# A new issue order, with new engine choices, for a fused attention and two-MLP kernel

## The chip, the cores and the metric

The kernel runs on one core of one Trainium2 chip. The metric is the device time of that core in microseconds (us). The core's engines work side by side, each through its own queue in order: TensorE (PE in the profile), with its weight loads shown apart (PEld), VectorE (DVE), ScalarE (ACT), GpSimd (POOL), and SyncE (SP), which here issues every DMA.

## The reference

Attention with a threshold on the scores, then two dense blocks on the 2304 tokens. Everything is float32.

```python
# q, k, v: (4, 8, 576, 64)
scores = scale * (q @ k.T)
thresh = max(scores, -1) - tau
scores = where(scores >= thresh, scores, -1e9) - max
attn = exp(scores) / (sum(exp(scores)) + 1e-9)
x = attn @ v                          # -> x: (2304, 512)
# block 1: 512 -> 2048 -> 512
h = x @ w_in
g = (a0 + a1*h + a2*h^2 + a3*h^3) / (1 + |b0||h| + |b1|h^2 + 1e-6)
x = g @ w_out
# block 2: 512 -> 1024 -> 1024 -> 512
out = (((x @ w1) * (x @ w2)) @ w3) @ w_out2
```

## The kernel before

**Numbers in pairs.** Most products keep float32 accuracy by splitting each operand into a float16 head and a float16 remainder and doing three float16 matmuls in place of one. So after most results stand two elementwise steps: one that makes the head (`copy`, a cast or a scaled copy from one input), and one that subtracts the head from the value to make the remainder (`rest`, two inputs, both in SBUF).

**Work.** The kernel lists 2431 events in Python: loads, attention steps for 16 pairs of heads in two halves each (`qk`, `top`, `thr`, `below`, `drop`, `exp`, `recip`, `p_hi`, `p_lo`, `p_t`, `pv`, `x_split`), weight preparation (`raw_w`, `conv_w`, `square_w`, `norm_w`, `split_w`, `w_product`), and for nine groups of 256 tokens the first block (`mlp1`: per eighth `h_product`, `act_h`, `num`, `den`, `inv`, `quotient`, `y_product`) and the second (`mlp2`: `ab_product`, `a_copy`, `c_mul`, `o_product`, `o_store`). Many events are Python generators that stop between their steps, so that another event's instructions can come in between.

**The order is written out by hand.** `ORDER` (lines 31 to 234) is a text of 4124 entries. Each number calls the next step of that event, so the entry's place is its place in the queue of each engine that it uses, SP's included. A letter behind the number sets the engine of a step that may run on more than one: a is ACT, v is DVE, p is POOL; with no letter the step has DVE or a fixed engine.

```python
        for token in ORDER.split():
            n = int(token.rstrip("apv"))
            eng[0] = token[len(str(n)):]
            if n not in gens:
                fn, args, *_ = events[n]
                gens[n] = fn(*args)
            if gens[n] is not None:
                next(gens[n], None)
```

**The free steps.** Four helpers read that letter. `copy` (lines 285 to 294) makes heads and scaled copies, on ACT (L287, L289) or on POOL or DVE (L291, L293). `tt` (L303) is the two-input subtract, add or multiply of `p_lo` (tile hl), `split_w` (wp), `den` (A), the last step of `quotient` (gg from A and r) and the last of `c_mul` (gg from U), on POOL or DVE. `small` (L306) is the two-column arithmetic of `thr` and `recip`. When the head was made with a scale, `rest` is on DVE alone (L300). Only DVE and ACT of these three can read the matmul results, so `top`, `exp`, `num` and the like have a fixed engine.

**The lines that the prediction names.** DVE: L625, L628, L631 are the three integer steps of `conv_w` on a raw weight tile; L784, L786 `num`; L802, L804, L806 the first three steps of `quotient`, followed by the multiply at L303 that may go to POOL; L460 `top`; L492 the masking after `exp`. ACT: L473 `below`, which needs `thr`; L772, L776, L779 `act_h`; L794, L796 `inv`. PE: L480 `drop`, which adds the mask that `below` made; L451 `qk`; L765 `h_product`; L822 `y_product`, which reads gg; L929 `ab_product`; L961 `o_product`. Buffers are few: two each of the tiles U, A and r, three of gg, nine of G (which holds scores, heads and raw q and k).

Of the kernel before, what the change touches and what calls it, by code (L numbers as in the profile page):

```python
# [31 lines left out]
7 0 1 3 12 92 18 2 4 5 13v 22 8 94p 20v 10 15 24 26 27v 6 31 9 14 9 29 9 35 11a 33 17 37 17 11 39 53  # L32
40v 16a 19 40 17 55 42 23 16 42a 48 44p 57 28 48a 59v 61 50p 46 21 63 64 21 68 66 52 21 70 96 25 32
25 72p 72 25 74 98 74a 36 79 100 76p 30 30 102p 77 103 30 105 107 34 41 111 79p 81p 109 34 113 34
128 83 115v 65 115 38 116 237 129 116a 38 122 118p 38 122a 131 124p 120 45 43 85 43 133p 135 43 137
67 69 67 239a 67 139 87a 126 311 141 142 87 73 89 144 166 146v 146 154 47 73 47 148 47 71 80 170 71
148a 71 150p 172 73 132 90a 174 152 176v 154a 168v 90 179 73 155p 178 84 157 181 75a 82 82 82 183
134 185 149 134 187 134 241 189v 136 140 189 86 78 86 138 191 88 243 196 244 191a 246v 86 250 192p
88 151 248 158 151 194 151 88 143 95 143 143 88 99 252 91a 160 160 160 167 254 93 159 97 256 97 153
97 257 101 308 145 202 101 259p 161a 161 101 147 196a 156 104 259 162 49 198p 204 261 205 261a 207v  # L40
200 310 267 263p 164 104 164 211 310 267a 265 209 310 268p 213 169 316 104 217 169 51 169 104 51 54
51 175 58 106a 318 108 318 318 215 56 324 58 218 56 307 56 220p 177 184 58 177 177 220 180 110 326
272 326 222 228 309p 326 58 222a 274 125 228a 224p 276 171 278v 173 281 230p 226 182 60a 186 186 285
# [12 lines left out]
486 488p 382 491 387 382 376 301p 301p 382 490 438v 490 395 438 492 384 524 495p 494 509 496v 439
390 303p 524 390 439a 303p 498 390 509 398 441p 403 299a 398 305a 398 299p 499 442 511 497 411 502
305p 511 498 500 504 501 444 406 518 406 505 406 509 449 507p 507 444a 419 514p 501 508 543 501 513
446p 413 516 413 543 516 501p 447 413 527 520 508a 568 489 408 421 510p 421 513a 392 421 515p 400
451 427 452v 424 530 517 454 519 416 455 519 457 521 527 459v 523p 459 519 525 530 526 519p 528 429  # L60
460 529 429 460a 429 531 462p 471 432 576 527 435 533 532p 435 578 546 545 435 534p 535 548 561 473
548 574 534 443 579 475 536 547 561 581p 536a 571 443p 549v 541 443p 537v 440 437 476 541v 440p 542v
440p 463 582 573v 478 437a 586 544 535 437p 584 538 445 587 538 445a 538 448 445p 453 538v 589 448p
450 453v 448p 453v 450a 479 450p 546 481 550 546 552 554 465 551p 456 603 555v 555 467 557 467 483
456p 468 605 456p 553 607 792 591 484 608p 553 557v 592v 558p 503 592 512 594 470v 470 503 461 461a
594p 464 503 461p 595v 564 522 556 464a 560 540 564 464p 556 522 610 539 556 611 567 540 556p 564
567 466 569p 469 559 466a 559 469a 466p 458 469v 522 458a 794 472 540 458p 794 572 559 794 472a 484
# [1108 lines left out]
```

## Time and profile before

| | |
|---|---|
| median of 3 runs | 1206.86 us (1206.33 to 1208.5) |
| the profiled execution's own time | 1207.75 us |
| its span, from first to last instruction | 1206.0 us |
| mean granted clock of TensorE, share of full speed | 0.95 |
| bytes moved by the DMA queue | 119.05 MB |

The span is 1.75 us short of the execution's time. The busy shares of the engines are means over stages that differ: the weights are prepared and attention starts in the first part, attention runs beside both dense blocks in the second, and the last part is nearly dense blocks alone.

### The profile page before, as it was taken

What the parts mean: (1) busy time and instruction counts of PE and PEld (TensorE: products, weight loads), DVE (VectorE), ACT (ScalarE), POOL (GpSimd) and SP (SyncE); (2) the same over time, 40 slices, a digit from 0 to 9 for tenths busy, and PEclk for the clock granted to TensorE, in tenths of its full rate; (3) what the DMA queues carried; (4) which work ended last, traced back from release to release, by engine and by line L of the source; (5) the groups of instructions that cost most, each with busy time, mean ns of one, the idle gap of its engine ahead of it and who ended that gap; (6) DMA issues with size and microseconds to landing.
All of it is one profiled execution on the core that took longest, in us unless ns stands there. A gap on an engine that the chain in (4) does not pass through costs nothing. (4 is left out here: it accounts for less than half of the span.)

```text
span 1206.0 us, 20660 instructions
## 1 busy us (share of the span) xinstructions
PE 994.5 (82%) x7889; PEld 729.4 (60%) x7892; DVE 920.5 (76%) x1674; ACT 732.5 (61%) x1208; POOL 502.3 (42%) x452
## 2 busy tenths in 40 slices
PE   3687655679787677998799899889999998998998
PEld 2333333554555456767666776667677677777675
DVE  5889899798999889688878998887878757277201
ACT  6647877957868577767656666665556435355211
POOL 1314475753576475234543453353444213123111
PEclk9999676899889799999999999999999999999999
DMA  7988954465435534573445155314412510000000
GB/s 219 278 235 227 231 142 127 91 146 170 105 80 120 126 78 107 116 177 96 96 82 126 21 111 117 67 27 89 101 29 41 85 36 1 18 18 2 18 18 18
DMA packets 201443, 120.37 MB, mean 100 GB/s; under 512 B 176384, under 2 KB 180480, under 8 KB 201344
## 3 DMA queue, kind: packets, MB, share of 16 engines
q1 hardware_dynamic: 201344, 119.05, 40.6%
q8 instruction: 62, 1.02, 0.3%
q14 instruction: 37, 0.30, 0.1%
HBM read 69.21 MB, written 7.34 MB: 63 GB/s over the span
## 5 line engine op out<-in xcount | busy, mean ns | idle before, releaser
L822 PE MATMUL y<-gg,wp 128*128 128x256 f16 x1728 | 213.6, 277 | 38.2 <-POOL gg L303 31.0
L822 PEld LDWEIGHTS <-wp 128*128 128x128 f16 x1728 | 169.4, 99 | 78.2 <-issue 56.3
L765 PEld LDWEIGHTS <-wp 128*128 128x128 f16 x1728 | 171.2, 100 | 74.4 <-DVE U L786 24.6
L765 PE MATMUL h<-xp,wp 128*128 128x256 f16 x1536 | 189.2, 281 | 32.5 <-DVE U L786 20.1
L929 PEld LDWEIGHTS <-wp 128*128 128x128 f16 x1728 | 168.4, 98 | 34.0 <-issue 10.9
L303 POOL TENSOR_TENSOR hl<-p,hl 128x576 f16<-128x576 f32 x81 | 114.8, 1419 | 114.5 <-ACT hl L287 107.3
L303 POOL TENSOR_TENSOR A<-A,r 128x512 f32<-128x512 f32 x67 | 88.7, 1324 | 148.5 <-ACT r L779 148.3
L303 POOL TENSOR_TENSOR gg<-A,r 128x512 f16<-128x512 f32 x64 | 89.0, 1391 | 140.5 <-DVE A L806 104.3
L451 PE MATMUL S<-raw 64*128 64x288 f32 x472 | 103.9, 475 | 17.6 <-DMA raw<-in_k_dram 9.6
L460 DVE TENSOR_REDUCE m<-S 128x1 f32<-128x576 f32 x132 | 95.3, 749 | 17.1 <-PE S L451 11.9
L961 PE MATMUL y<-wp,gg 128*128 128x512 f16 x432 | 99.6, 379 | 1.4 <-ACT A L289 1.1
L929 PE MATMUL h<-yy,wp 128*128 128x256 f16 x768 | 90.9, 275 | 2.4 <-ACT U L289 2.2
L490 ACT ACTIVATE p<-S,m 128x576 f32<-128x576 f32 x88 | 63.3, 737 | 40.9 <-DVE m L460 29.7
L513 ACT ACTIVATE p<-p,su 128x576 f32<-128x576 f32 x84 | 64.0, 767 | 38.1 <-DVE su L508 37.9
L451 PEld LDWEIGHTS S<-raw 64*128 64x128 f32 x472 | 56.0, 205 | 48.1 <-issue 18.9
L303 POOL TENSOR_TENSOR gg<-U,gg 128x512 f16<-128x512 f32 x33 | 39.3, 1192 | 106.2 <-ACT gg L287 96.5
L802 DVE SCALAR_TENSOR_TENSOR gg<-U,cf,r 128x512 f16<-128x512 f32 x72 | 64.5, 896 | 17.3 <-ACT r L796 17.0
L772 ACT ACTIVATE U<-h,cf 128x512 f32<-128x512 f32 x72 | 55.5, 771 | 36.5 <-DVE A L806 16.3
L492 DVE SCALAR_TENSOR_TENSOR p<-S,th,p 128x576 f32<-128x576 f32 x88 | 70.0, 813 | 8.9 <-ACT p L490 6.7
L303 POOL TENSOR_TENSOR wp<-cw,wp 128x512 f16<-128x512 f32 x51 | 70.0, 1384 | 15.3 <-ACT wp L287 9.4
L786 DVE SCALAR_TENSOR_TENSOR U<-U,cf,h 128x512 f32<-128x512 f32 x72 | 53.5, 746 | 24.7 <-ACT r L779 18.8
L804 DVE SCALAR_TENSOR_TENSOR A<-A,gg 128x512 f32<-128x512 f32 x72 | 67.3, 935 | 5.8 <-DVE gg L802 0.5
(186 smaller groups left out, 1887.4 us busy)
## 6 DMA issues: line engine op xcount, KB each, us to landing
rw<-in_moe_w_dram SPq DMA_DIRECT2D x32, 512.0 KB, 4.0
rw<-in_moe_w_out_dram SPq DMA_DIRECT2D x24, 512.0 KB, 4.1
raw<-in_k_dram SPq DMA_DIRECT2D x32, 288.0 KB, 3.5
wr<-in_v_dram SPq DMA_DIRECT2D x16, 576.0 KB, 4.3
rw<-in_moe_w_in_dram SPq DMA_DIRECT2D x16, 512.0 KB, 4.4
wr<-in_v_dram SPq DMA_DIRECT2D x16, 320.0 KB, 3.1
out_dram<-A SPq DMA_DIRECT2D x16, 256.0 KB, 2.0
raw<-in_q_dram SPq DMA_DIRECT2D x16, 160.0 KB, 3.4
```

What stands on the lines that cost most here:

```text
L303: (nc.gpsimd if eng[0] == "p" else nc.vector).tensor_tensor(o, x, y, op=op)
L451: nc.tensor.matmul(t[s][:, half, :HS], x[r, o:o + 128], y[r, keys], start=True, stop=True)
L460: nc.vector.tensor_reduce(st["m", b, c, blk][:, s:s + 1], t[:, :, :HS], axis=AX.XY, op=ALU.max, negate=True)
L490: nc.scalar.activation(x, t, AF.Exp, bias=m)
L492: nc.vector.scalar_tensor_tensor(x, t, st["th", b, c, blk][:, s:s + 1], x, op0=ALU.is_ge, op1=ALU.mult, accum_out=su)
L513: nc.scalar.activation(p, p, AF.Copy, scale=su)
L765: nc.tensor.matmul(t[:, e, :], w[:, a, o:o + 128], x[:, y, c, :], start=c + i == 0, stop=c == KD - 1 and i == 2)
L802: stt(p[:, 0, :], u, cf[:, 3:4], r, ALU.add, ALU.mult)
L804: stt(t, t, QC, p[:, 0, :], ALU.add, ALU.mult)
L822: nc.tensor.matmul(t[j // 2][:, j % 2, :], w[:, a, 128 * j:128 * j + 128], x[:, y, TG * e:TG * e + TG], start=f + e + i + j % 2 == 0, stop ...
L929: nc.tensor.matmul(t[:, TG * e:TG * e + TG], w[:, a, o:o + 128], x[:, y, c, :], start=c + i == 0, stop=c == KD - 1 and i == 2)
L961: nc.tensor.matmul(st["o", g][kt], x[:, a, m:m + 128], w[:, y, :], start=jp + e + i == 0, stop=jp == 3 and e == 1 and i == 2)
```

## The change

Nothing but the text of `ORDER` changes. All 2431 events and all 4124 entries stay, so every instruction's operation, tiles and shape stay. Two things differ.

**Places.** Entries stand a little elsewhere. Counted from the two listings, over the steps that keep their engine, a step moves by about 2 places in its engine's queue on average on PE, ACT and DVE and by 1 on POOL; the largest moves are 19 on PE, 49 on ACT, 85 on DVE and 14 on POOL. In SP's queue an issue moves by 1.7 places on average, by 21 at most. All queues keep their number of matmuls and DMAs.

**Engines.** Counted from the two listings, over the whole kernel:

| step | before: ACT / DVE / POOL | after |
|---|---|---|
| `p_lo` subtract (hl) | 0 / 63 / 81 | 0 / 82 / 62 |
| `den` add (A) | 0 / 5 / 67 | 0 / 19 / 53 |
| `quotient` last multiply (gg) | 0 / 8 / 64 | 0 / 50 / 22 |
| `c_mul` subtract (gg) | 0 / 3 / 33 | 0 / 20 / 16 |
| `split_w` subtract (wp) | 0 / 5 / 51 | 0 / 14 / 42 |
| `p_hi` head from a scaled value | 64 / 4 / 16 | 47 / 6 / 31 |
| `p_hi` first step (scaled copy or scaled head) | 128 / 4 / 12 | 123 / 12 / 9 |
| `split_w` head | 30 / 4 / 22 | 22 / 7 / 27 |
| `c_mul` head | 32 / 0 / 4 | 23 / 6 / 7 |
| `split_v` head | 15 / 0 / 1 | 10 / 4 / 2 |
| `x_split` head | 31 / 1 / 0 | 26 / 6 / 0 |
| heads and copies of `a_copy`, `split`, `scale_q`, `w_evac` | 67 / 10 / 9 | 65 / 13 / 8 |
| `thr` and `recip` | 0 / 109 / 51 | 0 / 105 / 55 |

The diff, cut to its ends (206 lines are replaced by 206):

```diff
 ORDER = """
-7 0 1 3 12 92 18 2 4 5 13v 22 8 94p 20v 10 15 24 26 27v 6 31 9 14 9 29 9 35 11a 33 17 37 17 11 39 53
-40v 16a 19 40 17 55 42 23 16 42a 48 44p 57 28 48a 59v 61 50p 46 21 63 64 21 68 66 52 21 70 96 25 32
...
-2402 2403a 2393v 2392 2392 2402 2394 2394a 2390 2404 2394p 2390 2390 2395 2390 2395 2404a 2395 2404p
-2395 2400 2400 2400 2405 2400 2405 2405 2405 2407a 2406v 2406 2407
+0 7 1 12 3 18 92 2 4 5 13v 20v 22 8 10 94a 15 24 26 27v 6 29 9 19 9 31 9 33 37 11v 35 11 39 53 17 14
+17 40p 40 17 42 21 23 42a 21 48 21 44p 48a 55 28 57 50p 46 16a 59v 63 52 16 61 66 25 32 25 64 68 25
...
+2390 2390 2390 2401 2402 2402 2401 2403a 2393v 2394 2394v 2394v 2395 2395 2404 2395 2404a 2395 2404v
+2400 2400 2400 2405 2400 2405 2405 2405 2406a 2407a 2406 2407
 """
```

## Rows read from the trace of the kernel before

**Rows 1.** Busy time of each engine over the span, from the page.

```profile
PE 994.5 (82%) x7889; PEld 729.4 (60%) x7892; DVE 920.5 (76%) x1674; ACT 732.5 (61%) x1208; POOL 502.3 (42%) x452
```

**Rows 2.** Stages: length, busy us of PE, PEld, DVE, ACT, POOL; granted clock; DMA.

```profile
0.00:478.00 478.00, 330.86 (x2140) 215.90 (x2144) 419.14 (x707) 339.75 (x609) 246.75 (x227) 0.88 0.59 155
478.00:840.00 362.00, 327.31 (x2910) 251.42 (x2910) 296.76 (x584) 234.35 (x364) 151.24 (x137) 0.99 0.43 93
840.00:1206.00 366.00, 336.30 (x2841) 262.08 (x2839) 204.55 (x385) 158.37 (x237) 104.31 (x89) 1.00 0.16 34
```

**Rows 3.** Longest wait of DVE, 0 to 478: total us, times, longest.

```profile
DVE su L306 <- ACT p L495: 6.6, 5, 3.3
```

**Rows 4.** Longest waits of PE, 0 to 478.

```profile
PE S L480 <- ACT x L473: 39.3, 16, 9.7
PE y L822 <- POOL gg L303: 13.7, 7, 2.7
```

**Rows 5.** Longest waits of PE, 840 to 1206.

```profile
PE y L822 <- POOL gg L303: 10.2, 11, 1.8
PE h L765 <- ACT r L779: 5.3, 3, 2.8
```

**Rows 6.** Line 303 alone by stage: us busy (instructions) of DVE, POOL.

```profile
0.00:478.00 478.00, 11.71 (x12) 188.82 (x136) 0.88 0.59 155
478.00:840.00 362.00, 2.47 (x3) 120.29 (x90) 0.99 0.43 93
840.00:1206.00 366.00, 11.04 (x9) 91.53 (x71) 1.00 0.16 34
```

**Rows 7.** Line 303 on DVE: ns shortest/median/longest.

```profile
L303 DVE TENSOR_TENSOR gg<-A,r x8: 673/692/1640, 217.4 to 1072.8; 128x512 f16<-128x512 f32 x8
L303 DVE TENSOR_TENSOR A<-A,r x5: 1161/1298/1408, 873.5 to 1096.8; 128x512 f32<-128x512 f32 x5
L303 DVE TENSOR_TENSOR hl<-p,hl x3: 758/758/1044, 209.2 to 228.4; 128x576 f16<-128x576 f32 x3
```

**Rows 8.** Single-input heads: two by shortest/median/longest ns, one group.

```profile
L291 DVE CAST wp<-cw x4: 420/862/1372, 162.3 to 245.4; 128x512 f16<-128x512 f32 x4
L291 POOL CAST wp<-cw x22: 600/650/1487, 143.2 to 443.7; 128x512 f16<-128x512 f32 x22
...
L287 ACT ACTIVATE wp<-cw 128x512 f16<-128x512 f32 x30 | 18.0, 620 | 0.3
```

**Rows 9.** Timeline of POOL and of DVE, 701 to 703: start us, us.

```profile
701.23 1.70 POOL L303 TENSOR_TENSOR gg<-A,r 128x512 f16<-128x512 f32 x1 [2.09 <-DVE A L806]
...
701.92 1.56 DVE L804 SCALAR_TENSOR_TENSOR A<-A,gg 128x512 f32<-128x512 f32 x1
```

**Rows 10.** DVE lines, 0 to 478: busy us, mean ns.

```profile
L628 DVE SCALAR_TENSOR_TENSOR cw<-rw,cw 128x512 int32<-128x512 int32 x72 | 68.6, 952 | 2.0
L631 DVE SCALAR_TENSOR_TENSOR cw<-rw,cw 128x512 int32<-128x512 int32 x72 | 64.0, 890 | 1.8
L625 DVE TENSOR_SCALAR cw<-rw 128x512 int32<-128x512 int32 x72 | 50.3, 698 | 7.1 <-DMA rw<-in_moe_w_in_dram 3.6 <-DMA rw<-in_moe_w_dram 2.8 <-DMA rw<-in_moe_w_out_dram 0.8
...
L806 DVE SCALAR_TENSOR_TENSOR A<-U,cf,A 128x512 f32<-128x512 f32 x22 | 23.7, 1075 | 0.6
```

**Rows 11.** DVE lines, shortest/median/longest ns over the whole span.

```profile
L628 DVE SCALAR_TENSOR_TENSOR cw<-rw,cw x72: 669/693/1750, 17.3 to 409.4; 128x512 int32<-128x512 int32 x72
L631 DVE SCALAR_TENSOR_TENSOR cw<-rw,cw x72: 671/692/1740, 19.6 to 410.6; 128x512 int32<-128x512 int32 x72
L625 DVE TENSOR_SCALAR cw<-rw x72: 404/422/1501, 16.8 to 408.0; 128x512 int32<-128x512 int32 x72
L806 DVE SCALAR_TENSOR_TENSOR A<-U,cf,A x72: 731/752/1844, 186.5 to 1113.4; 128x512 f32<-128x512 f32 x72
L306 DVE TENSOR_SCALAR th<-m,d x58: 207/228/1327, 13.4 to 961.4; 128x2 f32<-128x2 f32 x44, 128x1 f32<-128x1 f32 x14
```

More of the change, by code (lines that the diff above doesn't have):

```diff
@@ new lines @@
+821 668 671 668 812 823 832 668 633 735 835 633 835 838 838 677 635a 846 674 674 841 674 633 659a
+846p 846v 841a 731 677 638a 688 841p 688 641 688 850 631 691 643 632 677 643 634p 643 636 649 844
+665 637 677 639 667 669v 695 640p 672 695 697 673 640 695 642 816 680a 850p 850p 844v 676 682 844v
+678 697 681 642p 644p 646v 683 697 662 685v 685 646 687a 645 817a 690 701 651 694 817 697 739 694a
+703 743 705 696p 710 707v 647 700a 710 699 702 650 648 712 706 648 712 714v 714 744 716a 736v 1186
+692 652a 736 724 706 652 655 724p 706 719 729 725p 660 704 729a 660 660 754 709 728 664 729p 726 670
@@ new lines @@
+901p 964 1000p 1074 1010 1032 909 960 901p 1032 1003 1032 1035 1003 1011p 969 904 1035 1038p 904a
+1011 1003 1022 1012a 904p 1051 1017 1023 1042 1022 1024p 1051 1042 1022 909p 1026 1022v 1027 1014
+1054 1025 1045 1054 1015 909p 1025 1028 1123 1045 1058 1054 1030p 1025 1058 1061p 1046 1045 1119
+1064 1047 1045p 1077 972 1064 1119 1077 1067 1077 1048 1030 1080 1083p 1031a 1048 1080 1017a 1033
+1086 1018p 1096 1086 1067 1034 1020 1067 1096 1067v 1090 1120 1048 1090 1099 1070 1262 1090 1099
+1070 1103 1090p 1122 1103 1099 1070 1189 1049 1122 1106p 1036 1122 1050v 1093 1037 1053 1128v 1037
@@ new lines @@
+1044 1039 1109 1424 1125 1109 1125 1052 1112 1131 1112 1055 1040a 1056 1057 1093 1112 1112v 1059
+1040 1192 1114 1060v 1060 1066 1602 1071 1066a 1062v 1063 1117 1068v 1192 1131 1072 1372 1069 1135
+1076 1141 1073 1075v 1078 1135 1093 1076 1141 1078 1079v 1089 1144 1079 1135 1085 1148 1115 1135p
+1085a 1148 1065 1115 1144 1087v 1124a 1091 1144 1088 1115 1092v 1199a 1196 1121 1094 1095 1196 1097
+1081p 1041 1082 1151p 1084 1154 1098v 1098 1209 1202 1100a 1154 1101 1138 1157 1202p 1202p 1043a
+1102 1209 1157 1157 1127 1157v 1107 1129 1130 1215a 1132v 1133 1104 1134 1108v 1108 1136 1105 1137
@@ new lines @@
+1241 1179v 1179 1672 1180 1181a 1223 1421 1182 1241 1224 1184 1226 1229 1188 1227v 1230 1229 1230
+1232v 1232 1233a 1242 1190v 1222 1190 1238 1235 1244 1238a 1243 1236 1239p 1245v 1244 1246 1248
+1247v 1250 1185 1249 1240 1250v 1234p 1234p 1221 1250v 1319a 1251p 1269 1187 1675 1187 1251 1252a
+1319 1221 1254 1611 1237 1271 1221 1273 1276 1255 1237 1274v 1278 1276 1237 1237 1278 1259 1279v
+1279 1281a 1286 1283 1286a 1427 1253 1288v 1261a 1263 1253 1261 1290 1253 1285 1265 1257a 1256 1265
+1257 1265 1429a 1270 1374a 1268 1268 1253 1268 1270 1260a 1268 1260 1268 1291 1258 1272 1374 1258
@@ new lines @@
+1603 1287 1275 1608 1275 1272 1677 1287 1293 1272 1295 1277p 1298 1266 1337 1297v 1289 1298 1289
+1292 1289 1337 1292 1300 1321 1294p 1280 1300 1304 1280 1267v 1296 1282 1302p 1304 1296 1282 1322a
+1282 1282v 1481 1324 1306 1299 1306 1284 1299 1306 1284 1299 1311p 1302 1299v 1309 1284 1309a 1308
+1301 1313 1308 1310p 1301 1313 1326 1609 1312 1316 1320 1303a 1605 1316 1305 1320 1316 1331 1307
+1316v 1301 1323 1327 1318 1323 1325 1329p 1323 1318 1325 1340 1331 1606 1318 1328p 1342 1333 1371
+1342 1330 1333 1330 1371 1340 1334v 1332 1340 1332 1346 1344v 1332 1347 1354 1348 1347 1332p 1334
@@ new lines @@
+1349 1354 1341 1336a 1349 1341p 1353 1335 1349 1343p 1356 1335 1349v 1356 1359 1356 1352 1359 1373
+1361p 1352 1350 1373 1373 1351v 1376 1314 1355 1378v 1742 1364 1376 1380 1338 1380 1335 1364 1353
+1339 1315a 1345 1352 1355 1426 1357v 1357 1383 1363 1383 1426 1383 1366 1383p 1379 1431a 1366 1388
+1613 1315 1366 1614 1366v 1388 1381 1382 1386 1363p 1365p 1358p 1367 1368 1384v 1387 1368 1360 1386
+1362 1390 1390 1368 1387 1390 1385 1395v 1389p 1401 1389 1397 1392 1385 1396 1392 1396a 1375 1391v
@@ new lines @@
+1474a 1472 1536 1474 1546 1488 1536 1476a 1548 1551 1476 1549v 1488 1552 1540 1551 1552 1509 1491
+1554v 1554 1491 1494 1509 1491 1494 1560 1497v 1564 1512 1500 1515 1537 1500 1515 1512 1503 1512
+1503 1518p 1529 1539a 1503 1539 1521 1529 1566 1503p 1521 1567 1570 1560p 1550 1523 1532 1569p 1532
+1523 1561p 1506 1532 1523 1506 1555a 1535 1572 1523p 1550 1557 1526 1535 1553 1558 1526 1570 1553
+1553 1556 1506 1556 1542p 1538p 1541 1559p 1526 1541 1572 1571 1562 1544 1573p 1562 1544 1592 1573
+1544 1579 1544v 1575a 1571 1579p 1565 1547 1576 1563 1581p 1574 1547 1565 1574 1578 1582 1574 1565
@@ new lines @@
+1751 1696 1673 1756 1715v 1700p 1673 1717 1702p 1674 1701 1900 2143 1701a 1753 1701v 1758 1754p 1707
+1703 1756 1676a 1676 1718 1799a 1724 1758 1759v 1704 1759 1726 1761a 1720p 1704 1727v 1766 1721v
+1710 1763 1729 1723 1799 1704 1765 1707 1729 1730v 1730 1704 1732a 1771 1713a 1733 1710 1773 1775
+1778 1746 1766p 1768p 1739 1716 1780 1716v 1776p 1855 1716v 1735 1778 1719 1741a 1770 1743 1747v
+1719 1780 1719 1782v 1782 1741 1719 1788 1745 1722 1745 1745 1748 1788a 1722 1748 1748 1725 1728a
+1748 1783a 1748 1750 1785 1790p 1792 1725 1787 1750 1731 1731a 1736 1752 1731v 1804 1752 1738 1755
@@ new lines @@
+1738 1752 1755 1767 1679a 1805 1757p 1807 1767 1811 1809v 1760 1679 1734 1760 1811 1769 1734 1762
+1812 1957 1734 1762 1734 1762 1794 1740a 1812 1762p 1740 1772 1772 1814p 1737a 1826 1795a 1814 1737
+1821 1795 1764 1828 1784 1829 1769 1769 1831v 1784 1833 1816p 1821v 1774v 1857p 1833 1823p 1777 1801
+1777 1817 1786 1764 1779 1819 1786 1779 1786 1824 1764 1779 1834 1791p 1801 1779v 1793 1834 1781
+1793 1836v 1789 1781 1803 1789 1800 1803 1781 1796 1803 1818 1796 1808p 1796 1818 1810 1796v 1810
+1836 1806 1843 1798 1806 1820 1838p 1798 1813 1820 1820 1835 1822 1802p 1813 1825p 1835 1822 1827
@@ new lines @@
+1984 1924p 1985 1988 1931 1987v 1990 1988 1946a 1914 1990 1973a 1954 1991v 1974 1991 1936 1997 2002
+1956a 1958 1956 1914 2004 2024 1966 2005v 2007 1993v 1997p 1999v 1961 2007 1977a 1966 1961 1979p
+1961 1914 1964 1926 1980 1964 2008p 1976 1943 1964 1943 1964 1964 2025 2008 1948 2010a 1948v 1986
+1948v 2000 2027 1969 1986 2011 1969 1969 1972 1914 2031 2021 1972 1975p 1926 1936a 1994 1926 1936p
+1978 1926 2028 1996 1978 2006 2030v 2033 1981 1989 2022v 1938 1981 1989 1938 1981 1989 1938 1981v
+1995p 1938 1992 1950 1992 1998 1950 2031 1998 2017 2033 2034v 2034 2001 2041 2001 1950 2019a 2001
@@ new lines @@
+1950 1953a 2019 2006 2001v 1953 1955a 2088 2009 1955 2012 2026 2012 2009 2090 2026 2009 2092 2095
+2013 1983 2015v 2093p 2029 2095 1983 2018 2032 2018 2003 2032 2096 2003 2020 2029 2029 2096 1983
+2035v 2098p 2003 2098 2037 2020 2046 2104 2020 2037 2020v 2014 2040 2046 2036a 2016 2040 2016 2040
+2066 2049 2040v 2049 2038 2066 2049 2052 2099a 2039 2052 2045 2069 2101 2069 2023 2047 2069 2043
+2048 2051 2023 2050v 2055p 2102 2074p 2057 2072 2057 2051 2043 2053 2041p 2060 2042p 2023 2060 2043
+2077 2077 2044 2060 2086 2060v 2053 2063 2072 2063 2054p 2080 2080 2063 2080 2086 2080v 2054 2106
@@ new lines @@
+2089 2089 2091 2106 2089 2091 2061 2094v 2109 2061a 2056p 2058 2097 2062p 2148 2059 2110 2108 2108
+2112 2083 2097 2111 2113p 2108 2083 2111 2115 2104p 2100 2105p 2116 2145 2100 2114p 2100 2145 2117
+2100v 2083 2117 2115 2103 2151a 2120 2103 2064 2120 2120 2103 2120v 2065 2116 2148 2087 2118v 2118
+2124 2129 2154 2154a 2123 2130 2123 2067 2154p 2068v 2070 2132p 2123 2126a 2070 2081 2133 2071v 2071
+2128a 2133 2131 2135v 2135 2136a 2084 2119p 2121 2157 2107 2122 2124a 2134 2138 2157 2082a 2134
+2125p 2139 2157 2134 2157 2140 2137a 2160 2073v 2075 2137 2085a 2147 2160 2082 2149 2165a 2162 2150
@@ new lines @@
+2152 2155 2076 2162 2153v 2156 2155 2156 2174 2168 2174 2168a 2168v 2078 2171 2079 2079 2158p 2158
+2159a 2141 2127 2164 2169 2161 2164a 2171 2170 2166p 2171 2142 2175 2172 2142 2188 2167 2173v 2176
+2175 2188 2176 2178v 2178 2184 2171 2194a 2180v 2144 2184v 2186v 2179a 2181 2191 2146a 2163 2146
+2177 2191 2177 2197 2183 2197a 2187 2189 2182 2197p 2182a 2363 2190 2192v 2182p 2193 2363 2193 2195v
+2185 2195 2196a 2185 2198 2185 2199 2200 2204 2185 2206a 2206 2199 2199 2199 2201 2205a 2207 2203
+2205 2368 2203 2208 2217 2202a 2208 2208 2202 2209 2210 2209 2209 2217 2209 2209 2210 2368 2211 2211
@@ new lines @@
+2212 2364 2211 2212 2218 2213v 2224 2218 2219 2214 2219 2214 2224 2218 2215 2215 2220p 2245 2215
+2221 2245 2215v 2225 2225 2216 2226 2225 2216 2226 2221 2227v 2231 2222 2228 2222 2228 2222 2231
+2222v 2229 2216 2232 2229 2223 2233 2364 2233 2229 2223 2229v 2246 2223 2246 2247 2230 2246 2247
+2230 2232 2248v 2232 2249 2238 2249 2238 2234v 2235 2235 2236 2230 2236 2252 2236 2236v 2239 2252
+2239 2240 2239 2240 2237 2241v 2237 2242 2237 2242 2259 2243 2243 2243 2369 2250 2253 2243p 2259
+2250 2253 2250 2244 2253 2250v 2244 2254 2255p 2254 2244 2256 2251 2256 2273 2257 2257 2251 2257
@@ new lines @@
+2257v 2273 2258 2275a 2258 2260 2260 2261 2274 2260 2261 2262v 2274 2263 2263 2283 2276 2264 2283
+2264 2264 2278 2264v 2265 2265 2278 2266a 2251 2280a 2258 2276a 2265 2276v 2279 2267a 2268 2285v
+2279 2269 2281 2277 2269 2284 2269 2271 2270a 2284 2270 2288 2286 2295 2286a 2281p 2281p 2288 2286v
+2289 2290a 2289 2296 2277 2291 2297 2277 2297 2297 2282 2299 2277 2299 2282 2291a 2299 2282 2291p
+2282 2298a 2299 2299 2287 2287 2298 2287 2287 2362 2292 2292 2292 2292 2300 2294a 2293v 2293 2294
+2300 2307 2301 2302 2301 2307 2301 2302 2303v 2314 2308 2304 2309 2314 2304 2309 2308 2305 2308 2369
@@ new lines @@
+2305 2310p 2305 2328 2305v 2311 2311 2328 2315 2312 2315 2316 2306 2315 2306 2316 2317v 2312 2306
+2318 2312 2321 2318 2312v 2329 2319 2321 2329 2319 2329 2319 2313 2331p 2319v 2313 2322 2332 2330
+2313 2322 2323 2320 2322 2323 2320 2332 2330 2324p 2335 2325 2325 2335 2326 2326 2342 2326 2326v
+2336 2342 2333 2336 2337 2336 2327 2333 2338p 2327 2333 2339 2333v 2320 2339 2337 2327 2343 2340
+2334 2343 2344 2334 2343 2344 2345p 2340 2340 2346 2340v 2346 2334 2349 2349 2347 2347 2341 2350
+2347 2341 2350 2347v 2350 2351 2348 2370a 2351 2352p 2348 2371 2353 2378 2353 2354 2378 2354 2354
@@ new lines @@
+2341 2354v 2365a 2348 2366 2379 2366a 2366v 2355 2380a 2355 2355 2356a 2373 2357a 2358 2374 2374
+2367 2367 2367 2367 2379 2373 2381 2381a 2371p 2371p 2372 2375a 2381v 2372 2376 2372 2376a 2372
+2376v 2359 2377 2359 2359 2377 2361 2360a 2377 2408 2377 2385 2360 2382 2382 2382 2382 2409 2384a
+2383v 2383 2384 2409 2414 2411a 2414 2415 2416a 2415 2410 2417 2417a 2419 2417v 2419 2410 2420 2412
+2412a 2420 2412v 2413 2413 2413 2418 2413 2418 2418 2418 2424 2425 2425 2424 2426a 2421v 2422 2396
+2427 2396 2427a 2422p 2422p 2427v 2423 2398a 2423 2423 2423 2428 2428 2428 2428 2386 2430a 2429v
@@ L232 @@
+2429 2430 2387 2387 2386 2397 2388a 2389 2397 2391 2399 2399a 2389p 2389p 2392 2399v 2391 2392 2390
+2390 2390 2390 2401 2402 2402 2401 2403a 2393v 2394 2394v 2394v 2395 2395 2404 2395 2404a 2395 2404v
+2400 2400 2400 2405 2400 2405 2405 2405 2406a 2407a 2406 2407
 """
```

290 lines of the change are left out of this document (94 added, 196 removed).

## The prediction

> **What bounds the kernel now.** I read the page's busy line first, then the busy time by stage, then the waits of DVE and of PE in each stage, and last the durations on line 303 and of the DVE instructions that run beside it. No engine is full over the span: PE is busy 82%, DVE 76%, ACT 61%, POOL 42% [rows 1]. A mean over the span hides three stages, so I cut both listings where 30% and 65% of PE's matmul work has been issued; in the trace of before these places fall near 478 and 840 us. From 0 to 478 DVE is the fullest: 419.14 of 478 us, 88%, with PE at 330.86 (69%) and a granted clock of only 0.88 [rows 2]. The 59 us in which DVE is idle there are scattered: its longest wait in sum is 6.6 us in 5 times [rows 3]. PE's long waits in this stage, 39.3 us of `drop` for `below` and 13.7 us of `y_product` for gg [rows 4], stand behind work that DVE or POOL does late. So I take DVE to set the pace of the first stage. From 478 to 840 PE is at 327.31 of 362 us (90%), DVE at 296.76 (82%); from 840 on PE is at 336.30 of 366 (92%), DVE at 204.55 (56%) [rows 2]. There PE sets the pace, and what it loses it loses in short waits, the largest of them 10.2 us in 11 times for the gg that POOL makes [rows 5].
>
> **The change part by part.** It removes and adds no instruction; it moves 101 two-input steps of line 303 from POOL to DVE (19 hl, 14 A, 42 gg of `quotient`, 17 gg of `c_mul`, 9 wp), and some thirty single-input heads from ACT to POOL and DVE.
>
> *What a moved step costs DVE.* On DVE, line 303 takes 0.692 us for gg and 0.758 for hl in the median [rows 7]. For A only five rows exist, 1.161 to 1.408 us, all beside POOL; the lower bound is the 0.673 of gg, which has the same 512 elements, the upper the 1.298 of the median [rows 7]. I take 0.69, since the row of the same size that ran alone is the nearest. On POOL the same line takes 188.82 us for 136, 1.39 us each [rows 6].
>
> *What a removed step gives DVE back.* POOL does not work beside DVE for nothing. In the timeline POOL starts a subtract at 701.23 that lasts 1.70 us, until 702.93; DVE's L804, begun at 701.92, lasts 1.56 us and ends just after it [rows 9], more than twice the 0.692 of a two-input step of this size in the median [rows 7]. The `conv_w` steps show the same over the first stage: L628 has a mean of 0.952 us against its shortest of 0.669, L631 0.890 against 0.671, L625 0.698 against 0.404, each 72 times, and L806 1.075 against 0.731, 22 times [rows 10, 11]. The excess is 72 x (0.283 + 0.219 + 0.294) + 22 x 0.344 = 57.3 + 7.6 = 65 us of DVE time. POOL did 136 instructions of line 303 in that stage [rows 6], so one of them holds DVE for about 0.48 us. That is a mean of what collided, and its bounds are 0 (the steps left on POOL collide with the newly arrived ones instead, which read two tensors of SBUF too) and the full 1.39 us of the instruction. Even a two-column step of `thr` that takes 0.228 us lasted up to 1.327 [rows 11].
>
> The Trainium skill (SBUF — State Buffer, section "SBUF: two separate sides") says that GpSimd and those VectorE instructions that read two SBUF tensors lock one port pair for a whole instruction and that the loser blocks fully. The pair of instructions at 701 us agrees. By that rule taken to its end each removed POOL step would give DVE back its whole 1.39 us, and the first stage below would come out at -14 us; by my mean of 0.48 it comes out at +13. This is the first rival.
>
> *First stage.* 30 of the steps leave POOL (10 hl, 3 A, 8 gg, 9 wp) and 29 arrive on DVE: 9 x 0.758 + 20 x 0.69 = 20.6 us. Ten or so heads and scaled copies arrive as well (`split_v`, `split_w`, `x_split`), at 0.42 us for a 512-element cast that ran alone [rows 8], and some two-column steps, in all about 7 us. Sum +27.6. Given back: 30 x 0.48 = 14.4. DVE's load rises by 13 us, to 432; the ends are +28 (nothing given back) and 27.6 - 30 x 1.39 = -14. If DVE keeps its 59 us of idle time, the stage becomes 13 us longer. But the order brings some relief: entries of `drop` that stand closer behind their `below` than that step's duration, by the matmuls between them, fall from 40 to 30 in the two listings, and remainders made on DVE land 0.7 us sooner than on POOL. I let that take 5 us of idle time: **+8**, ends -14 and +28.
>
> *Second stage.* 32 leave POOL, 33 arrive: 9 x 0.758 + 24 x 0.69 = 23.4, other steps about 9, given back 32 x 0.48 = 15.4. DVE goes from 297 to 314 us of 362, 87%; PE with 327 remains the fuller one. What covers the added work is DVE's idle 65 us there. If that cover is gone, that is, if DVE's steps come late to a PE that has only two buffers of U, A and r ahead, the ends are 0 and +12. I take **+2**.
>
> *Third stage.* 39 leave POOL, among them 22 of the 23 multiplies of `quotient`. DVE goes from 205 to at most 205 + 39 x 0.69 + 2 = 234 of 366 us (64%), which costs nothing. The gg that PE waits for comes 1.39 - 0.69 = 0.7 us sooner, on 11 waits 7.7 us. But the new listing also places `y_product` and `o_product` closer behind their gg: in the last quarter of the matmul work, steps of `o_product` with fewer matmuls between them and their gg than the producer lasts were 6 and are 13, those of `y_product` were 15 and are 9. I count half: **-4**, ends -8 and +3.
>
> *Moves at no cost.* ACT loses 51 steps of about 0.62 us [rows 8]; ACT at 61% is not the bound in any stage [rows 1, 2], so nothing follows. Fifteen more `p_hi` heads go to POOL at about 0.65 us [rows 8]: POOL is at 52% in the first stage [rows 2] and has lost more than it gets; what covers them is that idle half. The DMA issues keep their number; SP's queue is reordered by 1.7 places on average, so a transpose may stand one issue later, and the DMA engines are busy 59% at most [rows 2]. In the first entries the loads of tau, a and b go ahead of the first v load; that is a microsecond at most of a first wait. The last two output copies both run on ACT, in place of one each on ACT and DVE; the first of them can run while PE does its last matmuls. I cost all of these at nothing.
>
> **Sum.** 8 + 2 - 4 = +6 us on the profiled execution: 1207.75 + 6 = 1213.75. The median of the runs shown is 0.9 below the profiled execution, so about 1213.
>
> **The rivals.**
>
> *The port rival, on the other side.* The price of a POOL step to DVE decides the first stage. It breaks even at 27.6 / 30 = 0.92 us per step removed. For a dearer price speak the 1.70 and 1.56 us pair [rows 9] and the longest rows of 1.75 us [rows 11]; against it that medians lie within 0.03 us of the shortest [rows 11], so most DVE instructions are not held. With the price at 1.2 the first stage is 27.6 - 36 - 5 = -13, the second 0, the third -4: 1207.75 - 17 - 0.9, about 1190.
>
> *The latency rival, also faster.* DVE would not be the pace of the first stage but the chain from subtract to transpose to the next matmuls would. Then a third of the 53 us of the two waits in [rows 4] goes with the shorter lead: -17 + 8, with the third stage -4, about 1194. Against it: DVE's longest wait is 6.6 us of 478 [rows 3].
>
> *No change.* DVE's idle 59 us take the 13 us in and the third stage loses nothing: 1205 to 1209.
>
> *DVE becomes the bound in the second stage as well.* For it speak 87% against PE's 90%, with shallow buffers. It gives +18 in the first stage, +12 in the second, 0 in the third: about 1237.
>
> **How the numbers follow.** The forecast (1209 to 1222) has 0.34, the port rival 0.28, the latency rival 0.12, no change 0.14, the double bound 0.12. A measurement of this kernel tells 0.2% (2.4 us) from no change. So faster has 0.28 + 0.12 = 0.40, same 0.14, slower 0.34 + 0.12 = 0.46; the forecast is the likeliest single case. The range has to hold cases of both signs: it runs from the port rival's 1190 to 1232, below the double bound's middle; beneath it I leave about 0.1, above it about 0.1. The forecast's own range is 1209 to 1222.
>
> **What would show it.** Right: DVE busy near 960 us over the span (920.5 + 13 + 17 + 39 x (0.69 - 0.48) + 2) and near 432 in the part that does the first 30% of the matmuls; POOL near 378 (502.3 - 101 x 1.39 + 24 heads of 0.65); mean of L628, L631 and L625 lower, but by less than a tenth of a us each; the PE wait of `y_product` for POOL's gg in the third stage down from 10.2 us to below 3. Wrong on the port price: DVE's busy time in the first stage at or below 419 though it does 29 more subtracts. Wrong on the pace: DVE's load up as said, but its idle time in the first stage down from 59 to 40 us or less. Wrong in the second stage: DVE above 90% there and PE waits for U or gg grown.

## The result: 0.9% faster, where 0.5% slower was forecast

The changed kernel takes 1196.9 us (median of 4 runs, 1195.8 to 1197.25) against 1206.69 for the kernel before beside it: a ratio of 0.9914 [0.9897, 0.9932]. The profiled execution took 1197.16 us with a span of 1195.4, 10.6 us less than before. So the time lies in the range on record, but the forecast had the wrong sign: 6 us slower on the profiled execution was forecast.

The page's busy line of the changed kernel answers to [rows 1].

```profile
PE 988.0 (83%) x7890; PEld 728.4 (61%) x7892; DVE 973.5 (81%) x1802; ACT 699.9 (59%) x1157; POOL 388.9 (33%) x375
```

DVE does 128 instructions more and is 53 us longer busy, and the kernel is faster all the same. The stages, cut again where 30% and 65% of the matmul work has been issued, answer to [rows 2]: length, busy us of PE, PEld, DVE, ACT and POOL, granted clock, DMA.

```profile
0.00:470.00 470.00, 329.35 (x2164) 218.06 (x2167) 427.45 (x751) 330.72 (x596) 207.07 (x204) 0.88 0.62 158
470.00:830.00 360.00, 321.44 (x2882) 247.55 (x2881) 322.59 (x635) 217.64 (x337) 124.52 (x118) 1.00 0.43 96
830.00:1195.40 365.40, 337.25 (x2846) 262.75 (x2844) 223.45 (x418) 151.57 (x227) 57.32 (x55) 1.00 0.16 32
```

These cuts are rounded. For a finer cut I matched the instructions of each kernel with those of before, in order, so that every stage holds the same share of the matmul work. By that matching the first stage ends 9.9 us earlier, the second is 2.3 us shorter and the third 1.6 us longer: -10.6 in sum. Cut by the number of weight loads alone, the three come to -10.0, +0.6 and -1.2, so the signs of the last two are not settled. Forecast were +8, +2 and -4. The gain is made in the first stage; the granted clock there is 0.88 in both kernels.

PE's longest waits there answer to [rows 4].

```profile
PE S L480 <- ACT x L473: 31.7, 11, 12.4
PE y L480 <- ACT x L473: 16.9, 6, 9.4
...
PE y L822 <- POOL gg L303: 7.3, 5, 2.2
```

`drop` waits for `below` 48.6 us in its two forms; before it was 39.3 for the first of them [rows 4] and 12.6 for the second:

```profile
PE y L480 <- ACT x L473: 12.6, 6, 4.0
```

The wait of `y_product` for POOL's gg fell from 13.7 [rows 4] to 7.3. DVE's longest wait in that stage was 6.6 us [rows 3] and is now 3.5:

```profile
DVE m L460 <- PE S L451: 3.5, 5, 1.3
```

The third stage's longest waits of PE answer to [rows 5]. POOL's gg has gone from 10.2 us to 1.9, and 8.9 us for DVE's gg stand in its place, so the wait for gg has not become shorter. The wait for U rose from 3.1 us to 6.9.

```profile
PE y L822 <- DVE gg L303: 8.9, 9, 1.9
PE h L765 <- DVE U L786: 6.9, 7, 1.6
PE y L822 <- POOL gg L303: 1.9, 1, 1.9
```

Line 303 by stage (busy us of DVE, then POOL) answers to [rows 6], and its shortest, median and longest durations on DVE to [rows 7]. The A step, of which before had five rows of 1.16 us and more, takes 0.684 in the median: the lower bound was right.

```profile
0.00:470.00 470.00, 36.53 (x43) 152.03 (x107) 0.88 0.62 158
470.00:830.00 360.00, 27.30 (x33) 76.27 (x57) 1.00 0.43 96
830.00:1195.40 365.40, 35.82 (x49) 43.19 (x32) 1.00 0.16 32
```

```profile
L303 DVE TENSOR_TENSOR gg<-A,r x50: 676/691/1695, 203.8 to 1104.3; 128x512 f16<-128x512 f32 x50
L303 DVE TENSOR_TENSOR hl<-p,hl x22: 744/758/864, 29.9 to 943.0; 128x576 f16<-128x576 f32 x22
L303 DVE TENSOR_TENSOR A<-A,r x19: 678/684/694, 256.5 to 1069.0; 128x512 f32<-128x512 f32 x19
```

The `conv_w` lines in the first stage (busy us, mean ns, idle before) answer to [rows 10]. Two of the three means fell, L628 by 0.08 and L625 by 0.13 us, and that of L631 rose from 0.890 to 0.916.

```profile
L631 DVE SCALAR_TENSOR_TENSOR cw<-rw,cw 128x512 int32<-128x512 int32 x72 | 65.8, 916 | 1.8
L628 DVE SCALAR_TENSOR_TENSOR cw<-rw,cw 128x512 int32<-128x512 int32 x72 | 62.7, 872 | 2.1
L625 DVE TENSOR_SCALAR cw<-rw 128x512 int32<-128x512 int32 x72 | 41.0, 570 | 5.4 <-DMA rw<-in_moe_w_in_dram 2.7 <-DMA rw<-in_moe_w_out_dram 1.4 <-DMA rw<-in_moe_w_dram 1.3
```

### The profile page after: what moved, and what is told of

It reads as the page before. It is cut to its first block, busy times and chain, and to the rows that moved or that the text cites. A ratio compares the mean times of both kernels' runs of the same rounds, so it can differ in the third digit from the quotient of the medians.

```text
span 1195.4 us, 20542 instructions
## 1 busy us (share of the span) xinstructions
PE 988.0 (83%) x7890; PEld 728.4 (61%) x7892; DVE 973.5 (81%) x1802; ACT 699.9 (59%) x1157; POOL 388.9 (33%) x375
## 5 line engine op out<-in xcount | busy, mean ns | idle before, releaser
L765 PE MATMUL h<-xp,wp 128*128 128x256 f16 x1536 | 192.5, 284 | 32.8 <-DVE U L786 17.7
L303 POOL TENSOR_TENSOR A<-A,r 128x512 f32<-128x512 f32 x53 | 74.1, 1400 | 187.4 <-ACT r L779 152.2
L303 POOL TENSOR_TENSOR hl<-p,hl 128x576 f16<-128x576 f32 x62 | 88.2, 1423 | 88.9 <-ACT hl L287 65.0
L451 PE MATMUL S<-raw 64*128 64x288 f32 x472 | 99.0, 468 | 14.9 <-DMA raw<-in_k_dram 8.8
L794 ACT ACTIVATE r<-A,lnb 128x512 f32<-128x512 f32 x72 | 51.7, 718 | 35.9 <-POOL A L303 22.4
L877 PE MATMUL h<-cw 128*128 128x512 f32 x128 | 64.5, 648 | 9.6 <-DVE cw L631 5.5
L961 PEld LDWEIGHTS <-gg 128*128 128x128 f16 x432 | 41.3, 98 | 46.8 <-issue 2.1
L806 DVE SCALAR_TENSOR_TENSOR A<-U,cf,A 128x512 f32<-128x512 f32 x72 | 67.1, 933 | 2.0
L786 DVE SCALAR_TENSOR_TENSOR U<-U,cf,h 128x512 f32<-128x512 f32 x72 | 53.6, 746 | 18.6 <-ACT r L779 15.7
L784 DVE SCALAR_TENSOR_TENSOR U<-h,cf,U 128x512 f32<-128x512 f32 x72 | 53.7, 745 | 18.4 <-ACT A L776 12.8
```

Source lines behind the costliest of these rows:

```text
L303: (nc.gpsimd if eng[0] == "p" else nc.vector).tensor_tensor(o, x, y, op=op)
L451: nc.tensor.matmul(t[s][:, half, :HS], x[r, o:o + 128], y[r, keys], start=True, stop=True)
L765: nc.tensor.matmul(t[:, e, :], w[:, a, o:o + 128], x[:, y, c, :], start=c + i == 0, stop=c == KD - 1 and i == 2)
L806: stt(t, u, cf[:, 3:4], t, ALU.add, ALU.subtract)
L877: nc.tensor.matmul(t, st["cw", ("w3", m, j // 4)][:, o:o + 128], st["cw", ("wo2", j)], start=j == 0, stop=j == 7)
L961: nc.tensor.matmul(st["o", g][kt], x[:, a, m:m + 128], w[:, y, :], start=jp + e + i == 0, stop=jp == 3 and e == 1 and i == 2)
```

## The experiments

All kernels change only the text of `ORDER`. Three things can be set apart: the **places** (the order of the numbers), the engine letters of the 320 **two-input** steps of line 303 (296 on POOL before, 195 after; 60 more `p_lo` steps run on DVE alone, at L300), and the letters of all **other** free steps (heads, scaled copies, two-column arithmetic). Each time is compared with the kernel before on the same chip, whose medians lay between 1206.7 and 1207.6. A diff shows one stretch of some fourteen entries, its minus line from the kernel before unless said otherwise.

**Old places, all new letters.**

```diff
-561 581p 536a 571 443p 549v 541 443p 537v 440 437 476 541v 440p
+561 581v 536p 571 443p 549p 541 443v 537p 440 437 476 541a 440a
```

> The old places with the new engine of every step. Theory L (the engines make the gain: fewer two-input steps on POOL, so DVE is held less and its inputs come sooner): 1195 to 1200 us, DVE busy about 973, its idle time in the first stage near 42 us. Theory P (the new places make the gain, and the engines alone only load DVE): 1206 to 1216 us, idle time in the first stage near 59 us.

Measured: 1232.64 us, 1.0213 [1.0189, 1.0237]. The letters alone lose 2.1%.

**New places, all old letters** (here the minus line is the changed kernel's).

```diff
-586 448v 544 448v 437 478 573v 443 437v 437v 440 443p 467 440a
+586 448p 544 448p 437 478 573v 443 437a 437p 440 443p 467 440p
```

> The new places with the old engine of every step. Theory L: 1203 to 1210 us, as before. Theory P: 1190 to 1200 us, with DVE busy about 920 and less idle time in the first stage. If neither part alone gives the gain (the places fit the engines that they were written with), both e1 and e2 are at or above 1205.

Measured: 1257.91 us, 1.0425 [1.0401, 1.0449]. The places alone lose more. Neither half carries the gain; they fit each other.

**The change in the first 30% of the matmul work alone**: the changed kernel's entries up to there, then before's, each event's steps in before's order (the minus line is the changed kernel's).

```diff
-1034 1020 1067 1096 1067v 1090 1120 1048 1090 1099 1070 1262 1090 1099
+1034 1020 1067 1096 1067v 1090 1048 1090 1099 1070 1262 1090 1099 1070
```

> New places and engines in the first 30% of the matmul work alone, old ones behind. If the gain is the first stage's, as the times of equal steps in the two traces say (8 of the 10 us are there by 400 us): 1197 to 1200 us. If a good start is lost again behind it because a stage that PE sets takes it back: 1203 or more.

Measured: 1200.42 us, 0.9944 [0.9925, 0.9963].

**The change behind the first 30% alone**, joined in the same way.

```diff
-872 971 965p 890 989 977 1191 977 881 977 984 991 967p 981
+872 971 965p 890 989 977 977 881 977 984 991 967p 981 967p
```

> Old places and engines in the first 30%, new ones behind. If the gain is the first stage's: 1203 to 1207 us. If the later stages carry it: 1197 to 1200 us. My recorded sum had +2 and -4 for these stages, 1205.

Measured: 1210.28 us, 1.0017 [1.0001, 1.0033]. The first stage brings most of the gain by itself; the rest without it brings none.

**New places, two-input letters new, all other letters old** (here and in the next four diffs the minus line is the changed kernel's).

```diff
-574 541a 435 581v 549p 435 551p 582 542v 465 448 476 586 448v
+574 541v 435 581p 549v 435 551p 582 542v 465 448 476 586 448p
```

> New places, the two-input steps of line 303 on their new engines, every other free step back on its old one (the heads back on ACT). Theory H (the gain is ACT's relief from heads, which DVE waited for): 1203 to 1212 us, and DVE's waits for ACT in the first stage back at 20 us or more. Theory S (the gain is the two-input steps that left POOL): 1195 to 1200 us. Theory F (places fit all engines together, and any part undone costs): 1205 to 1225.

Measured: 1238.21 us, 1.0253 [1.0234, 1.0272].

**New places, two-input letters old, all others new.**

```diff
-295a 292p 288a 290v 379 369 487 288v 295p 353 297v 361 305 297v
+295a 292v 288a 290v 379 369 487 288p 295p 353 297v 361 305 297p
```

> New places, the two-input steps back on their old engines (296 on POOL), every other free step on its new one. Theory S: 1205 us or more, since POOL's 1.4 us steps come late and hold DVE again. Theory H: 1195 to 1202 us. Theory F: 1215 to 1255, next to the 1258 with all old engines on the new places.

Measured: 1216.54 us, 1.008 [1.0066, 1.0094]. The new places with the heads written for them lose 0.8% as long as the two-input steps stay on POOL. The 127 changed two-input letters (the two directions net to 101) are worth 1216.5 - 1196.9 = 19.6 us.

**New letters, places shuffled.** Neighbours that share no tile are swapped at random, so that a step stands 0.5 to 1.8 places from where it stood in its engine's queue on average and 14 at most, less than in the change itself. SP's queue, which issues the DMAs, is shuffled too.

```diff
-0 7 1 12 3 18 92 2 4 5 13v 20v 22 8
+12 7 1 18 92 3 2 0 4 13v 22 24 26 5
```

> The new engines; the new places shuffled at random by swaps of neighbours that share no tile, a mean move of 1.2 places on PE and ACT and 1.8 on DVE, some half of what stands between the two listings. Theory F (the time hangs on places that fit the durations): 1203 to 1220 us with the same busy times. If only the loads and the rough order count: 1195 to 1200 us.

Measured: 1417.52 us, 1.1742 [1.1718, 1.1766], about ten times the largest loss that was expected. DVE's longest waits over the span; the longest of the changed kernel over its span is 22.7 us:

```profile
DVE m L460 <- PE S L451: 51.8, 28, 5.1
DVE gg L802 <- ACT r L796: 40.1, 28, 4.3
```

So an order is not judged by how far its steps move on average. It is one shuffle, and why its swaps cost just so much was not followed up.

**New places, all 320 two-input steps on DVE**, others as changed.

```diff
-350 282a 275p 277a 350 288 485 282p 284 363 415 388a 485 277p
+350 282a 275v 277a 350 288 485 282v 284 363 415 388a 485 277v
```

> New places; all 320 two-input steps of line 303 on DVE, so POOL has single-input work and two-column steps alone. It measures what a POOL step takes from DVE. At my recorded price of 0.48 us each: DVE busy 973 + 195 x (0.69 - 0.48) = 1014 us. At 0.75: 961 us, and L628, L631, L806 at their shortest duration in nearly all instructions. If the holding has another cause than POOL's two-input steps: 1080 us or more. Time by theory F: 1205 to 1235.

Measured: 1197.65 us, 0.9919 [0.9901, 0.9936], as fast as the change. The page's busy line and two of the lines of [rows 11]:

```profile
PE 996.4 (83%) x7892; PEld 731.7 (61%) x7892; DVE 986.3 (82%) x1997; ACT 699.2 (58%) x1157; POOL 121.3 (10%) x180
...
L628 DVE SCALAR_TENSOR_TENSOR cw<-rw,cw x72: 669/692/1035, 17.2 to 400.0; 128x512 int32<-128x512 int32 x72
L806 DVE SCALAR_TENSOR_TENSOR A<-U,cf,A x72: 732/752/1032, 179.8 to 1105.5; 128x512 f32<-128x512 f32 x72
```

DVE has taken on 195 more instructions of about 0.70 us, 136 us in sum, and is busy 986.3 - 973.5 = 12.8 us longer: over the whole span a POOL step took 0.70 - 12.8 / 195 = 0.63 us of DVE (an estimate), more than the recorded 0.48. The longest L628 fell from 1.750 us [rows 11] to 1.035. Counting the DVE instructions that last over 0.6 us longer than the shortest of their line and shape in any run, there are 135 before, 102 in the changed kernel, 2 here and none in the old order with all these steps on DVE. The 2 stand beside a head of `split_v` (L293, 1152 elements) that POOL makes from one input; in the changed kernel the longest L806 is such a case (timeline: start us, us):

```profile
672.72 4.22 POOL L293 TENSOR_SCALAR vh<-wr,vs 128x1152 f16<-128x1152 f32 x1
...
674.00 3.26 DVE L806 SCALAR_TENSOR_TENSOR A<-U,cf,A 128x512 f32<-128x512 f32 x1
```

**The changed kernel, with the two-input steps of its first stage on DVE** (106 steps; behind it 89 stay on POOL). The edit is the one above, up to there.

```diff
-350 282a 275p 277a 350 288 485 282p 284 363 415 388a 485 277p
+350 282a 275v 277a 350 288 485 282v 284 363 415 388a 485 277v
```

> The kernel after with the remaining 106 two-input steps of its first 30% on DVE too, the rest as in after. Theory R (a two-input step on POOL takes from DVE about what DVE itself takes for it, so moving it is free and lands sooner): 1190 to 1196 us, the first stage 3 us shorter than in after as with no two-input step on POOL at all. If a place list loses by any change of engines (theory F): 1198 or more.

Measured: 1190.66 us, 0.9865 [0.9853, 0.9878], the fastest of all, below both kernels. Its busy line, and the `conv_w` lines of its first stage:

```profile
PE 992.5 (83%) x7890; PEld 731.1 (61%) x7892; DVE 972.4 (82%) x1908; ACT 699.7 (59%) x1157; POOL 241.1 (20%) x269
...
L628 DVE SCALAR_TENSOR_TENSOR cw<-rw,cw 128x512 int32<-128x512 int32 x72 | 51.1, 711 | 1.9
L631 DVE SCALAR_TENSOR_TENSOR cw<-rw,cw 128x512 int32<-128x512 int32 x72 | 50.8, 708 | 1.4
```

DVE does 106 instructions more than in the changed kernel and is busy 1.1 us less. L628 and L631 have come from 0.872 and 0.916 us to 0.711 and 0.708.

**The kernel before with all two-input steps on DVE**, places and other letters untouched.

```diff
-350 275p 277a 292 485 363 282p 388a 420 295 388 485 284 277p
+350 275v 277a 292 485 363 282v 388a 420 295 388 485 284 277v
```

> Old places, all 320 two-input steps on DVE, every other step on its old engine. Theory R: DVE busy in the first stage within 6 us of the 419 of before though 136 more steps run on it; 1190 to 1208 us. By my recorded price of 0.48 us DVE's busy time in the first stage would be 419 + 136 x (0.70 - 0.48) = 449 us and the kernel 1225 or more. Theory F: 1215 or more with DVE's busy time unchanged and more idle time.

Measured: 1192.97 us, 0.989 [0.9875, 0.9905]. One rule applied to the old order gives as much as the whole change, or a little more, where the recorded price had 1225 or more. Its first stage, cut at 468, and L806 over the span:

```profile
0.00:468.00 468.00, 333.63 (x2165) 218.98 (x2169) 416.36 (x846) 342.50 (x613) 59.91 (x91) 0.88 0.60 159
...
L806 DVE SCALAR_TENSOR_TENSOR A<-U,cf,A x72: 731/752/755, 177.3 to 1099.9; 128x512 f32<-128x512 f32 x72
```

DVE does 846 instructions in 416.36 us, where before it did 707 in 419.14 [rows 2]; by the recorded price it would be 449. The longest L806 is 0.755 us, where it was 1.844 [rows 11].

**Old places, two-input letters new, others old.**

```diff
-538 448 445p 453 538v 589 448p 450 453v 448p 453v 450a 479 450p
+538 448 445v 453 538v 589 448p 450 453v 448v 453v 450a 479 450v
```

> Old places, the two-input steps on their new engines (195 on POOL), every other step on its old one. Theory R: 1195 to 1208 us. Theory F: 1212 to 1235 us.

Measured: 1203.69 us, 0.9963 [0.995, 0.9976].

**Old places, two-input letters old, others new.**

```diff
-561 581p 536a 571 443p 549v 541 443p 537v 440 437 476 541v 440p
+561 581v 536p 571 443p 549p 541 443p 537v 440 437 476 541a 440a
```

> Old places, the two-input steps on their old engines, every other free step (heads, thr, recip) on its new one. If it is the heads whose places and engines have to fit: 1220 to 1245 us, near the 1233 of all new engines on old places, with DVE waiting more for ACT and POOL in the first stage (23 and 1.5 us before). If the relief of ACT is a gain of its own: 1195 to 1206.

Measured: 1235.18 us, 1.0236 [1.0223, 1.025]. Taking load off ACT is no gain by itself: ACT is busy 700.5 us in place of 732.5 [rows 1], and the kernel is 28 us slower. In the first stage DVE's waits for ACT go from 23.1 us to 24.0 and those for POOL from 1.4 to 6.4; where the rest is lost was not traced.

**The runs side by side**, in us:

| places, other letters | two-input as before | two-input as changed | all two-input on DVE |
|---|---|---|---|
| old, old | 1207.4 | 1203.7 | 1193.0 |
| old, new | 1235.2 | 1232.6 | not run |
| new, old | 1257.9 | 1238.2 | not run |
| new, new | 1216.5 | 1196.9 | 1197.7; first stage only 1190.7 |

From the first column to the second, the two-input steps that leave POOL make it faster in every row: by 2.5 to 3.7 us on the old places, by 20 on the new ones. Down the first column, everything else in the change makes it slower. In the last column the first stage alone is worth more than all stages.

## Why the prediction was wrong

The table shows DVE in the first stage, matched as said above: where the stage ends, DVE's instructions (without its 12 or so short reads of an accumulator), busy us, idle us from its first instruction on (3 to 4 us after the start), how much of the idle time waits for ACT, and what ACT itself waits there for POOL. An end is known to about 1 us.

| kernel | end | DVE instr. | busy | idle | of it for ACT | ACT for POOL |
|---|---|---|---|---|---|---|
| before | 478 | 693 | 418.8 | 54.9 | 23 | 21.9 |
| new places, two-input as before | 474 | 703 | 419.4 | 51.1 | 22 | 28.2 |
| changed | 467 | 733 | 424.1 | 39.2 | 13 | 5.6 |
| changed, all two-input on DVE | 463 | 839 | 422.2 | 37.9 | 13 | 3.4 |
| old places, all two-input on DVE | 466 | 830 | 414.4 | 47.6 | 23 | 5.9 |

**The price of a POOL step was mis-sized** (0.48 us, "a mean of what collided"). By their shortest durations the steps that arrive in the first stage come to 26 us, near the 27.6 forecast. DVE's busy time rose by 5.3. So 20.7 us were given back, 0.69 us for each of the 30 that left. With all of the stage's two-input steps moved on the old places it is (136 x 0.70 + 4) / 136 = 0.73. These are estimates: neighbouring rows of DVE overlap a little, and with every row counted in full the two come to 0.59 and 0.62. The forecast had only the excess of four lines of DVE, 65 us; over all lines, each row against the shortest of its line, it is 104 us, so the other lines and the two-column steps were left out. This term put the first stage's load at +13 in place of +5, 8 us of the error. The price is still below the 0.92 at which load alone breaks even, so the port rival, at 1.2, was no better: the two-input steps cost DVE about the same on either engine, 0.7 us. POOL relieves DVE of little or nothing there.

The Trainium skill (SBUF — State Buffer, section "SBUF: two separate sides") has the pair of ports as an exclusive lock whose loser blocks for the other's whole instruction. The longest rows agree: 1.844 us of L806 fell to 0.755 in the old order once no two-input step ran on POOL; the 3.26 us above stand beside a single-input step of 4.22 us. As a mean over a stage the measured 0.7 us is about half of the 1.39 that the rule's end would give.

**The idle time was the larger error** ("I let that take 5 us of idle time"). It fell by 15.7 us, and 10 of these are waits for ACT. Counted from the start of the stage, as the 59 us of the prediction were, it fell from 58.9 to 42.5, just short of the recorded sign of a wrong pace, 40 us. From the second line of the table to the third only two-input letters differ: busy +4.7, idle -11.9, the stage 7 us shorter. At the same time ACT's waits for POOL fall from 28.2 to 5.6 us. Before, the longest of them were these:

```profile
ACT sq L638 <- POOL gg L303: 8.2, 3, 5.5
ACT x L473 <- POOL th L306: 7.2, 6, 2.6
ACT r L794 <- POOL A L303: 4.7, 4, 2.2
```

After, with gg gone from the list:

```profile
ACT x L473 <- POOL th L306: 3.8, 3, 2.6
ACT r L794 <- POOL A L303: 1.8, 2, 1.4
```

So the step that failed is "So I take DVE to set the pace of the first stage": DVE is the fullest engine, but its load alone does not set the length. Over the thirteen kernels other than the shuffled one, cut at the same number of weight loads, DVE is busy 412 to 424 us in this stage and idle 34 to 71 us: the length goes with the idle time.

What fills the idle time is in part argued: a two-input step that costs DVE the same on either engine but lands 0.7 us sooner, and not behind POOL's queue, would shorten the loops between DVE, ACT and POOL. That is close to the latency rival, with 1194 us the nearest of the five. The two rows that it named fell from 53.0 to 39.0 us, 14 of its 17, but the other form of `drop`'s wait rose from 12.6 to 16.9. How the waits add up along one loop was not traced, and the path by ACT is not shown on the old places: with all two-input steps on DVE its waits for ACT stayed at 23 us, and the 7 us came out of its other waits; with the letters of the change they rose to 27 us although ACT's waits for POOL fell to 9.8.

**Second and third stage.** Forecast +2 and -4, measured -2.3 and +1.6, neither clear of zero. In the second DVE is at 322.59 of 360 us, 90%, and PE's waits for gg there grew from 9.0 to 10.8 us, those of `h_product` for U from 6.4 to 7.4: the bound that the double-bound rival feared was touched, at a microsecond or two. In the third the wait for POOL's gg went as forecast, but 9 waits for DVE's gg took its place. They are all of `y_product`, whose close entries had become fewer by the prediction's count; `o_product`, whose close entries had become more, waits 0.2 us there. So the count of close entries did not tell where PE would wait. DVE's 973.5 us over the span lie above the 960 forecast: its load rose by 27 us in the second stage (17 forecast) and by 20 in the third (10 forecast), where it is less full: with the arrivals of the prediction, a step that left POOL gave back about 0.2 us there (an estimate). The run with POOL kept in these stages is 7 us faster than the one without. In the profiled executions the second stage is 6.6 us shorter with POOL and the third 1.8 us longer, where the first, the same order in both, differs by 2.8; so POOL still pays in the second, and in the third nothing is shown.

**Moves at no cost** was right only for the pair. Heads on new engines cost 2.4% on the old places, and with heads on their old engines the changed kernel takes 1238.2 us, 3.5% more. So the free time of ACT and POOL, the cover named for these moves, did not make them free. One cost is shown above: DVE's L806 beside a head on POOL lasted 2.5 us longer than its median. That a head comes late for its place is likely, but was not traced.

## What to carry to other kernels

Before giving a two-input step to POOL, compare DVE's busy time and not DVE's instruction count with and without it: in the stage where DVE is 88% busy, a POOL step took from it about as much as it saved, and it lands later. In this kernel such steps of the first stage could be moved where they stand, with a gain in both orders, while new heads or new places alone lost 2 to 4%: places and engines of that kind have to be tried together. And the fullest engine of a stage need not be its bound while it still idles a tenth of the time: ask what its idle time waits for, one engine further back.

## What was not expected of the hardware

POOL relieved DVE of little by doing two-input work over SBUF: in the old order 296 steps moved to DVE, some 207 us of work by themselves, raised DVE's busy time from 920.5 [rows 1] only to 956.9 us. In the first stage it even fell, by 4 us.

```profile
PE 992.7 (83%) x7889; PEld 730.4 (61%) x7892; DVE 956.9 (80%) x1970; ACT 732.9 (61%) x1208; POOL 108.9 (9%) x156
```

And one shuffle of the order by a place or two cost 17%, more than any choice of engines tried here.
